# Chunks 6 and 7 with their second layer in seven products, and q and k of units 12 to 23 split by GpSimd's transfers

## The chip, the core and the metric

The kernel runs on one core of a Trainium2 chip. The metric is the time of one execution on the device in microseconds (us). TensorE is called PE, VectorE DVE, ScalarE ACT, GpSimd POOL or Pool, SyncE SP in the profile, and so here.

## The reference

An attention with a narrow band and block summaries feeds a two-layer MLP. B, H, S, D = 4, 8, 768, 64; the MLP goes from 512 to 2048 and back to 512 columns.

```python
k_sum = k.reshape(B, H, nb, block, D).max(axis=3)          # block 32, nb 24
v_sum = v.reshape(B, H, nb, block, D).mean(axis=3)
scores_l = scale * q @ k.T, masked to |i - j| < 16
scores_s = scale * q @ k_sum.T + log(block)
a = softmax(concat([scores_l, scores_s]))
x = a @ concat([v, v_sum])                                  # per head, heads side by side
h = x @ w_in;  g = gelu(h) (erf);  out = g @ w_out          # 3072 tokens
```

## The kernel before, in words

Everything is written out by hand in one list, `ORDER`: each entry names a step with its numbers, a step issues its instructions on its engines' queues when the list comes to it, and each engine then works its own queue in order and waits for semaphores. So the list sets the order within an engine; entries of different engines run past one another.

**Precision.** TensorE multiplies f16. Every factor is held as a sum of two f16 parts (hi and lo), and a product is three matmuls: hi·hi, hi·lo, lo·hi. The hi part is a copy on ACT, the lo part a subtraction on DVE.

**Attention** runs in 24 units (four heads by 256 tokens). For a unit `load_q`, `load_k` fetch f32 tiles on SP's queue, `s_q_hi`, `s_k_hi` (ACT, L796, L739) and `q_lo`, `k_lo` (DVE, L805, L799) split them. k's parts lie in `k_hi[u % 2]` and `k_lo[u % 2]`, so unit u can fill its buffer only when `scores` of unit u-2 is done. Then `scores` (PE, L831, 48 small matmuls), `add_mask` (DVE, L851), `maximum` (an all-reduce over partitions on Pool, L860), `shift`, `exponent`, `s_p_hi`, `p_lo`, `values` (PE, L913), `sums` (PE, L929), and the division and split that give x.

**The MLP** runs in twelve chunks of 256 tokens. Chunks 0 to 3 do the first layer straight (`phase1`, 24 matmuls of 256 columns a step). Chunks 4 to 11 do it in pairs b = 2 to 5, with the seven products of Strassen's scheme (`sp b q n`, L1061, 12 matmuls of 256 columns, q a quarter of the 2048 columns): the sums of input blocks are `xsum`, the sums of weight blocks are made once by `wt_add`, `wt_hi`, `wt_lo` and stay in the tile `wt`. The second layer of chunks 0 to 7 is straight: `phase2 c i`, L1109 to L1111, eight steps a chunk, each 12 matmuls of 512 columns. The second layer of chunks 8 to 11 (pairs 4 and 5, `L2`) is in seven products too: `so b n q j`, L1297, 6 matmuls of 256 columns, 56 steps a pair. For those the hidden blocks are combined by `h_sum` and split by `h_hi`, `h_lo` (L1186, L1189) and the sums of `w_out` blocks are made by `t_sum`, `t_hi`, `t_lo` (L1231, L1236, L1260, L1263) between the steps of chunks 8 and 9, into tiles of attention that are free by then. Pair 5 keeps its combined hidden blocks in `wt`, whose weight sums nobody needs any more.

The end is `so 5 4 3 1`, its evacuation `o_out 5 1` (ACT, L1333) and a store `o_put` on SP's queue (L1337).

Of the kernel before, what the change touches and what calls it, by code (L numbers as in the profile page):

```python
# [16 lines left out]
ALU = mybir.AluOpType  # L17
# [41 lines left out]
M16_ROOM = 0  # L59
# [14 lines left out]
L2 = (4, 5)  # L74
N_FILL = 16
# [50 lines left out]
s_q_hi 10, wt_add 0 0, g_lo 2 0, load_vs 8, v_hi 8, exponent 9, load_k 10, fetch_v 2 0, v_lo 8, load_v 11, phase1 3 4,  # L126
s_k_hi 10, sums 8, g_lo 2 3, scores 11, add_mask 11, load_v 10, wt_add 0 1, values 8, put 0 1, q_lo 10, wt_add 0 2,
phase1 3 5, gelu 3 2, load_vs 10, k_lo 10, norm_take 8, s_p_hi 9, p_lo 9, phase1 3 6, maximum 11, wt_hi 0, norm_cross
8, sums 9, scores 10, norm_rec 8, norm_spread 8, load_q 12, load_k 12, gelu 3 6, store 1 1, norm_mult 8, gelu 3 5,
prep_v 2 0, load_vs 11, x_hi 8, add_mask 10, v_hi 10, values 9, norm_take 9, wt_lo 0, norm_cross 9, g_hi 3 6, put 1 1,  # L130
shift 11, g_hi 3 2, gelu 3 4, s_k_hi 12, v_lo 10, wt_add 2 0, x_lo 8, g_hi 3 4, k_lo 12, s_q_hi 12, fetch_v 2 3,
norm_rec 9, phase1 3 1, q_lo 12, phase1 3 0, v_hi 11, v_lo 11, exponent 11, g_lo 3 2, prep_v 2 3, phase2 2 1, k_sums 2
0, norm_spread 9, s_p_hi 11, load_k 13, gelu 3 1, load_q 13, norm_mult 9, maximum 10, phase1 3 7, load_v 12, phase2 2
3, prep_k_end 2 1, g_lo 3 4, s_q_hi 13, p_lo 11, x_hi 9, shift 10, g_hi 3 1, wt_add 3 0, gelu 3 0, wt_add 3 1, q_lo
13, s_k_hi 13, g_hi 3 0, phase2 2 5, phase1 3 3, g_lo 3 0, wt_add 3 2, k_sums 2 1, wt_add 2 1, sums 11, norm_take 11,
g_hi 3 5, g_lo 3 1, load_vs 12, scores 12, exponent 10, load_v 13, values 11, norm_cross 11, phase2 2 7, wt_add 2 2,
s_p_hi 10, load_q 17, sp 2 0 1, add_mask 12, norm_rec 11, wt_hi 2, k_lo 13, x_lo 9, scores 13, p_lo 10, sums 10, gelu
3 7, load_vs 13, gelu 3 3, norm_spread 11, maximum 12, norm_mult 11, norm_take 10, values 10, sp 2 0 2, s_q_hi 17,
snap 2 0 1, q_lo 17, wt_lo 2, x_hi 11, store 2 1, v_hi 12, x_lo 11, v_lo 12, norm_cross 10, load_k 15, g_hi 3 3, g_lo
3 3, add_mask 13, shift 12, s_k_hi 15, maximum 13, g_lo 3 5, norm_rec 10, exponent 12, v_hi 13, load_q 15, norm_spread  # L140
10, s_q_hi 15, norm_mult 10, xsum 2 1, comb 2 0 0, phase2 2 0, phase2 2 2, phase2 2 4, put 2 1, s_p_hi 12, sp 2 1 1,
k_lo 15, p_lo 12, xsum 2 3, phase2 2 6, sp 2 1 2, xsum 2 2, sums 12, q_lo 15, load_k 14, xsum 2 4, shift 13, load_v
15, values 12, wt_add 4 0, xs_hi 2 1, xs_hi 2 2, g_hi 3 7, xs_hi 2 3, wt_add 4 1, snap 2 1 1, xs_hi 2 4, xs_lo 2 1,
load_vs 15, wt_add 5 0, wt_add 5 1, scores 15, store 2 0, phase2 3 0, g_lo 3 7, exponent 13, norm_take 12, wt_hi 3,
xs_lo 2 3, xs_lo 2 2, load_q 14, norm_cross 12, wt_lo 3, s_gelu 2 0 0, wt_add 4 2, wt_hi 4, phase2 3 2, s_p_hi 13,
norm_rec 12, sp 2 0 6, sp 2 1 6, s_k_hi 14, comb 2 1 0, wt_add 6 0, wt_add 5 2, xs_lo 2 4, wt_add 6 1, sg_hi 2 0 0,
snap 2 0 2, v_hi 15, sp 2 0 5, put 2 0, wt_lo 4, phase2 3 4, g_lo 3 6, wt_hi 5, sp 2 0 7, wt_add 7 0, k_lo 14, v_lo
15, norm_spread 12, snap 2 1 2, phase2 3 6, s_q_hi 14, sp 2 1 7, wt_add 7 1, wt_add 7 2, snap 2 0 3, wt_hi 7, store 3
0, p_lo 13, wt_add 6 2, load_k 17, v_lo 13, wt_hi 6, sp 2 0 4, s_gelu 2 0 2, wt_lo 7, comb 2 0 3, phase2 3 1, wt_lo 5,
load_v 14, wt_lo 6, sp 2 0 3, sg_hi 2 0 2, fetch_v 3 0, put 3 0, sp 2 1 5, load_vs 14, norm_mult 12, prep_v 3 0,  # L150
s_gelu 2 0 3, fetch_k 3 1, sg_lo 2 0 2, phase2 3 3, s_gelu 2 1 0, comb 2 0 1, sp 2 2 1, q_lo 14, load_q 16, sg_lo 2 0
0, s_gelu 2 0 1, s_k_hi 17, k_lo 17, sg_hi 2 1 0, add_mask 15, sg_lo 2 1 0, snap 2 1 3, values 13, snap 2 2 1, comb 2
1 3, s_gelu 2 1 3, sums 13, prep_k 3 1, sg_hi 2 1 3, scores 14, v_hi 14, sp 2 2 6, sg_hi 2 0 3, snap 2 2 2, sp 2 1 3,
sg_lo 2 0 3, load_k 16, v_lo 14, add_mask 14, comb 2 1 1, sp 2 1 4, norm_take 13, maximum 15, phase2 3 5, s_gelu 2 1
2, load_v 17, s_k_hi 16, sg_hi 2 0 1, s_gelu 2 1 1, sg_hi 2 1 1, maximum 14, sg_lo 2 0 1, sp 2 2 2, shift 15, comb 2 2
0, shift 14, norm_cross 13, s_q_hi 16, fetch_v 3 2, q_lo 16, exponent 14, sg_hi 2 1 2, s_p_hi 14, sp 2 3 2, phase2 3
7, norm_rec 13, load_q 18, exponent 15, sp 2 3 1, snap 2 3 1, sg_lo 2 1 3, norm_spread 13, k_lo 16, sg_lo 2 1 1,
fetch_k 3 0, sp 2 2 7, scores 16, p_lo 14, norm_mult 13, load_k 18, comb 2 3 0, values 14, sums 14, store 3 1, sg_lo 2
1 2, norm_take 14, s_p_hi 15, x_hi 12, sp 2 2 5, norm_cross 14, prep_k 3 0, snap 2 2 3, prep_k_end 3 0, sp 2 3 6,
phase2 4 0, snap 2 3 2, p_lo 15, x_hi 13, s_gelu 2 2 0, comb 2 2 3, sp 2 2 3, norm_rec 14, norm_spread 14, sp 2 2 4,  # L160
add_mask 16, norm_mult 14, comb 2 2 1, s_gelu 2 2 3, sp 2 3 5, values 15, s_gelu 2 3 0, scores 17, sg_hi 2 2 0, sums
15, load_v 16, sg_hi 2 3 0, maximum 16, sp 2 3 7, prep_v 3 2, phase2 4 2, sg_lo 2 2 0, s_gelu 2 2 1, fetch_k 3 2, x_lo
13, put 3 1, shift 16, exponent 16, snap 2 3 3, sg_hi 2 2 1, sp 2 3 4, norm_take 15, sg_lo 2 3 0, fetch_k 3 3, comb 2
3 3, prep_k 3 2, s_k_hi 18, norm_cross 15, x_lo 12, s_gelu 2 3 2, sp 2 3 3, sg_hi 2 2 3, s_p_hi 16, sg_lo 2 2 1,
s_gelu 2 3 3, load_vs 16, k_lo 18, sp 3 0 1, norm_rec 15, add_mask 17, sg_hi 2 3 2, comb 2 3 1, sp 3 0 2, norm_spread
15, sg_hi 2 3 3, norm_mult 15, s_q_hi 18, s_gelu 2 3 1, q_lo 18, load_vs 17, v_hi 16, sg_hi 2 3 1, phase2 4 4, v_hi
17, p_lo 16, sg_lo 2 3 1, phase2 4 6, v_lo 16, x_hi 15, maximum 17, k_sums 3 0, scores 18, fetch_v 3 1, s_gelu 2 2 2,
x_lo 15, sg_hi 2 2 2, store 4 0, sg_lo 2 2 3, shift 17, load_k 19, sums 16, load_v 18, xsum 3 1, load_q 20, xs_hi 3 1,
values 16, snap 3 0 1, phase2 5 0, sg_lo 2 3 2, xsum 3 3, fetch_v 3 3, s_k_hi 19, s_q_hi 20, exponent 17, v_lo 17,
xsum 3 2, comb 3 0 0, xs_hi 3 2, prep_k 3 3, norm_take 16, prep_k_end 3 1, sg_lo 2 2 2, sp 3 1 2, sp 3 1 1, prep_v 3  # L170
1, sg_lo 2 3 3, k_lo 19, k_sums 3 1, xs_lo 3 2, phase2 5 2, phase2 5 4, snap 3 1 1, sp 3 0 6, q_lo 20, comb 3 1 0,
s_p_hi 17, xsum 3 4, sp 3 1 6, phase2 5 6, put 4 0, xs_hi 3 4, load_q 19, xs_lo 3 4, load_v 19, xs_lo 3 1, snap 3 0 2,
add_mask 18, xs_hi 3 3, xs_lo 3 3, sp 3 0 7, maximum 18, prep_v 3 3, s_gelu 3 1 0, s_q_hi 19, snap 3 1 2, store 5 0,
shift 18, snap 3 0 3, norm_cross 16, load_k 20, sp 3 0 5, comb 3 0 3, norm_rec 16, exponent 18, load_vs 18, v_hi 18,
sp 3 0 4, norm_spread 16, p_lo 17, sp 3 1 7, norm_mult 16, phase2 4 1, s_k_hi 20, q_lo 19, scores 19, add_mask 19,
s_gelu 3 0 0, s_gelu 3 0 2, values 17, v_lo 18, sums 17, norm_take 17, norm_cross 17, norm_rec 17, put 5 0, maximum
19, sp 3 0 3, phase2 4 3, phase2 4 5, s_gelu 3 0 3, sg_hi 3 0 0, sg_lo 3 0 0, k_lo 20, shift 19, load_k 21, phase2 4
7, norm_spread 17, s_p_hi 18, comb 3 0 1, s_gelu 3 0 1, sg_hi 3 0 1, exponent 19, sp 3 2 1, p_lo 18, sp 3 1 5, s_k_hi
21, snap 3 2 1, snap 3 1 3, store 4 1, sums 18, norm_mult 17, load_q 21, values 18, s_q_hi 21, scores 20, k_lo 21,
norm_take 18, sp 3 2 6, phase2 5 1, load_vs 19, v_hi 19, sg_lo 3 0 1, comb 3 1 3, sp 3 1 3, sg_hi 3 1 0, snap 3 2 2,  # L180
s_p_hi 19, norm_cross 18, sg_lo 3 1 0, q_lo 21, load_v 20, add_mask 20, sg_hi 3 0 3, load_k 22, norm_rec 18, comb 3 1
1, sp 3 1 4, s_k_hi 22, maximum 20, s_gelu 3 1 1, sg_hi 3 1 1, k_lo 22, sg_lo 3 0 3, sp 3 2 7, v_lo 19, sp 3 2 2,
# [71 lines left out]
1  # L254
'''


SLOTS = {
    "f4k": (
        "0123020301321302310302320130310213021302321022013023313020301323012323130230102101312010320231302130"  # L260
        "212130"
    ),
    "g32": (
        "012301203223103123011323320131133012130213021322032100323012320130121032"
    ),
    "ks16": (
# [1185 lines left out]
```

## Time and profile before

| | us |
|---|---|
| median of 3 runs (562.19 to 562.35) | 562.32 |
| profiled execution, span | 560.5 |
| PE busy | 552.6 (99%) |
| DVE busy | 472.6 (84%) |
| ACT busy | 384.8 (69%) |
| Pool busy | 94.7 (17%) |

The span runs from the first to the last instruction that the profile shows; the median stands 1.8 us above it. The granted clock was 1.00, the level of 2.4 GHz, in every slice. Matmuls are pipelined, so a duration of one (379 ns for 512 columns) is longer than its share of PE's time; the time from one start to the next is what counts. The same holds in part for DVE and ACT.

### The profile page before, as it was taken

To read this page: it belongs to the slowest core of one execution; us is meant where nothing else is said; L and a number is where in the kernel's file an instruction comes from. 1 tells how busy PE (TensorE), PEld (TensorE's weight loads), DVE (VectorE), ACT (ScalarE), POOL (GpSimd) and SP (SyncE) were. 2 spreads that over 40 slices of the span, in tenths; PEclk is the share of its full clock that TensorE was granted. 3 is DMA by queue.
4 is the path that set the end of the run, shared out by engine and by line. 5 is a ranking of instruction groups with operands and counts; after the bars stand their busy time and mean duration, and the time that the engine had idled before them with its cause. 6 is when DMAs were issued, how large, how long until landed. Compare 5 with 4: busy or idle time off the path is not lost.

```text
span 560.5 us, 13994 instructions
## 1 busy us (share of the span) xinstructions
PE 552.6 (99%) x6011; PEld 402.2 (72%) x6011; DVE 472.6 (84%) x660; ACT 384.8 (69%) x665; POOL 94.7 (17%) x42
## 2 busy tenths in 40 slices
PE   8999999999999999999999999999999999999997
PEld 4568886585677666677766677665668788888886
DVE  4999999999999999979898768768689999667641
ACT  4689766768688997658878787795747664455521
POOL 2644030202412240031222211223000000000000
PEclk9999999999999999999999999999999999999999
DMA  8989545647554423424352043220000000001011
GB/s 320 396 274 389 189 154 191 266 130 207 158 163 116 146 64 107 144 81 139 91 148 90 28 130 115 63 65 2 22 19 1 20 1 2 2 1 48 1 48 57
DMA packets 29230, 64.30 MB, mean 115 GB/s; under 512 B 2800, under 2 KB 8688, under 8 KB 29168
## 3 DMA queue, kind: packets, MB, share of 16 engines
q1 hardware_dynamic: 28880, 63.06, 34.3%
q8 instruction: 47, 0.77, 0.6%
q10 hardware_dynamic: 288, 0.34, 0.2%
q14 instruction: 15, 0.12, 0.1%
HBM read 55.34 MB, written 6.29 MB: 110 GB/s over the span
## 4 chain that ended last, share of the span: by engine, by line
PE 76%; DVE 17%; DMA 3%; issue 2%; ACT 1%; SPq 0%; DVEq 0%
PE psy L1061 13%; PE pso L1109 9%; PE pso L1110 9%; PE pso L1111 9%; PE psz L1061 7%; PE psd_y L1297 4%; PE pso_y L1297 3%; PE pss_x L1297 3%; PE psx L1061 3%; PE psv L913 3%; PE psh L990 2%; PE psh L991 2%; PE psh L992 2%; PE pss L831 2%; DMA w_out_h<-in_vt_dram 2%
## 5 line engine op out<-in xcount | busy, mean ns | idle before, releaser
L860 POOL PARTITION_ALL_REDUCE m<-s x23 | 82.4, 3582 | 284.4 <-DVE s L851 114.2
L1109 PE MATMUL pso<-w_out_h,gg 128*128 128x512 f16 x256 | 97.1, 379 | 0.0
L1111 PE MATMUL pso<-w_out_h,gg 128*128 128x512 f16 x256 | 97.0, 379 | 0.0
L1110 PE MATMUL pso<-w_out_l,gg 128*128 128x512 f16 x256 | 97.0, 379 | 0.0
L1061 PEld LDWEIGHTS <-wt 128*128 128x128 f16 x768 | 74.7, 98 | 12.1 <-issue 0.6
L991 PE MATMUL psh<-xos,ww 128*128 128x256 f16 x256 | 69.8, 273 | 0.8 <-DVE xos L970 0.8
L990 PE MATMUL psh<-xos,ww 128*128 128x256 f16 x256 | 69.8, 273 | 0.1
L1061 PE MATMUL psy<-xos,wt 128*128 128x256 f16 x576 | 69.8, 273 | 0.0
L992 PE MATMUL psh<-xos,ww 128*128 128x256 f16 x256 | 69.8, 273 | 0.0
L1061 PEld LDWEIGHTS <-ww 128*128 128x128 f16 x576 | 56.0, 98 | 9.8 <-issue 0.2
L1111 PEld LDWEIGHTS <-gg 128*128 128x128 f16 x256 | 25.0, 98 | 30.5 <-DVE gg L1093 0.4
L1109 PEld LDWEIGHTS <-gg 128*128 128x128 f16 x256 | 25.0, 98 | 25.9
L1110 PEld LDWEIGHTS <-gg 128*128 128x128 f16 x256 | 25.0, 98 | 25.8
L1297 PEld LDWEIGHTS <-gg 128*128 128x128 f16 x384 | 37.6, 98 | 5.1 <-issue 0.3
L1072 ACT ACTIVATE ww<-psy 128x512 f32<-128x512 f32 x48 | 27.8, 588 | 13.7 <-PE psy L1061 10.9
L1189 DVE SCALAR_TENSOR_TENSOR gg<-h,gg 128x512 f16<-128x512 f32 x32 | 21.7, 684 | 11.1 <-ACT gg L1186 11.1
L1093 DVE SCALAR_TENSOR_TENSOR gg<-g,gg 128x512 f16<-128x512 f32 x32 | 22.7, 711 | 8.0 <-ACT gg L1089 7.9
L865 DVE TENSOR_TENSOR s<-s,m 128x1024 f32<-128x1024 f32 x21 | 25.5, 1217 | 4.3 <-POOL m L860 4.3
L990 PEld LDWEIGHTS <-ww 128*128 128x128 f16 x256 | 25.0, 98 | 4.2 <-issue 0.2
L992 PEld LDWEIGHTS <-ww 128*128 128x128 f16 x256 | 25.0, 98 | 4.1 <-issue 1.2
L991 PEld LDWEIGHTS <-ww 128*128 128x128 f16 x256 | 25.0, 98 | 3.8
L999 ACT ACTIVATE g<-psh 128x512 f32<-128x512 f32 x32 | 18.9, 593 | 11.4 <-DVE gg L1008 8.7
(192 smaller groups left out, 1273.1 us busy)
## 6 DMA issues: line engine op xcount, KB each, us to landing
v<-in_vw_dram SPq DMA_DIRECT2D x24, 512.0 KB
k<-in_kd_dram SPq DMA_DIRECT2D x20, 320.0 KB
gg<-in_w_in_dram SPq DMA_DIRECT2D x6, 1024.0 KB
q<-in_qd_dram SPq DMA_DIRECT2D x23, 256.0 KB
kp<-in_kp_dram SPq DMA_DIRECT2D x12, 392.0 KB
vb<-in_vb_dram SPq DMA_DIRECT2D x12, 384.0 KB
xos<-in_w_out_dram SPq DMA_DIRECT2D x4, 1024.0 KB
x32s<-in_w_out_dram SPq DMA_DIRECT2D x4, 1024.0 KB
```

Of the source, the lines that this page charges most:

```text
L860: nc.gpsimd.partition_all_reduce(out_ap=self.m32, in_ap=self.s32, channels=P, reduce_op=bass_isa.ReduceOp.max)
L865: nc.vector.tensor_tensor(out=self.s32, in0=self.s32, in1=self.m32, op=ALU.subtract)
L990: nc.tensor.matmul(ph[:, e, :], wh, xh, start=(k == 0), stop=False)
L991: nc.tensor.matmul(ph[:, e, :], wh, xl, start=False, stop=False)
L992: nc.tensor.matmul(ph[:, e, :], wl, xh, start=False, stop=(k == NCC - 1))
L1061: nc.tensor.matmul(ps[:, e, :], ws, xx, start=(first and e == 0 and k == 0 and m == 0), stop=(k == 1 and m == 2), skip_group_check=True,)
L1072: nc.scalar.activation(snaps[b, q, n], split8(acc[b, q, "y"]), AF.Copy)
L1093: nc.vector.scalar_tensor_tensor(out=g_part(o // 2, q, 1, fs), in0=g32t.pop((b, q, o)), scalar=SC_G, in1=g_part(o // 2, q, 0, fs), op0=ALU ...
L1109: nc.tensor.matmul(p, gh, w_out_h[:, f, :], start=(f == 0), stop=False)
L1110: nc.tensor.matmul(p, gh, w_out_l[:, f, :], start=False, stop=False)
L1111: nc.tensor.matmul(p, gl, w_out_h[:, f, :], start=False, stop=(f == NFC - 1))
L1297: nc.tensor.matmul(ps, g, ww_, start=(first and e == 0 and k == 0), stop=(e == 1 and k == 2), skip_group_check=True,)
```

## The change

- `STREAM = (3,)`: the second layer of chunks 6 and 7 (pair 3) is done by 56 steps `so 3 n q j` in place of 16 steps `phase2`. Their hidden blocks take the `h_` steps (`h_comb`, `h_gelu`, `h_sum`, `h_hi`, `h_lo`) in place of `comb`, `s_gelu`, `sg_hi`, `sg_lo`.
- Pair 3 comes before pair 4, whose first layer still needs the weight sums in `wt`, and the combined hidden blocks of pair 3 go into `wt`. So `ws` (4 steps) writes `wt` to DRAM beforehand, and `wr` (16 steps, 256 KB each) reads it back, slot by slot, as the steps `so 3` let go of it. The `w_out` sums are made earlier, staged in one tile and written to DRAM by `ts` (16); `t1_load` (2) and `tl` (12) read them for pair 3, `tr` (12) for pairs 4 and 5. All of these are on SP's queue.
- Units 12 to 23: `q_cast`, `k_cast` are transfers issued by Pool that convert f32 to f16 on the way; ACT writes the negated copy (`q_neg`, `k_neg`); `q_acc`, `k_acc` are transfers by Pool that add the f32 source to it, which leaves the lo part. They take the place of `load_q`, `load_k`, `s_q_hi`, `s_k_hi`, `q_lo`, `k_lo`. A new input `k96` holds k in rows padded to 96 columns; `k_sum` (ACT) writes the block maxima into `k_hi` after each cast.
- The accumulators of pair 3 lie in the `pso` bank and in `psh`; `mask16_sb` and `ks_f` move into a tile that is free early on; `ks16` has four buffers; the scratch for Pool's transfers doubles.
- The order is unchanged up to the 499th entry (the end of `v_lo 8`) and new from there on, with other buffer numbers in `SLOTS`.

The diff, cut; of the new order two places stand: from `scores 10` to shortly before `scores 12`, and the start of pair 4.

```diff
-M16_ROOM = 0
+M16_ROOM = 1
...
+STREAM = (3,)
...
+2 1, wt_add 0 2, norm_take 9, phase1 3 3, load_v 11, scores 10, x_hi 8, load_vs 10, maximum 11, g_hi 3 4, g_lo 2 3,
+load_vs 11, wt_hi 0, shift 11, wt_hi 3, norm_cross 9, add_mask 10, wt_lo 0, values 9, v_hi 11, q_acc 12, phase2 2 1,
+wt_lo 3, put 1 1, k_cast 12, v_hi 10, v_lo 10, norm_rec 9, norm_spread 9, norm_mult 9, k_cast 13, gelu 3 0, exponent
+11, g_lo 3 1, s_p_hi 11, g_hi 3 2, q_cast 13, k_neg 12, fetch_v 2 3, maximum 10, k_sums 2 1, g_lo 3 4, phase1 3 5,
+phase2 2 3, g_hi 3 0, k_acc 12, q_neg 13, p_lo 11, shift 10, k_sum 12, exponent 10, q_acc 13, phase1 3 7, v_lo 11,
+gelu 3 7, wt_add 7 0, wt_add 7 1, sums 11, wt_add 7 2, phase2 2 5, g_hi 3 7, x_lo 8, k_sums 2 0, g_lo 3 0, values 11,
...
+23, wr 3 3 1, sums 21, so 3 4 0 1, wr 3 0 2, wr 3 1 2, xsum 4 4, o_snap 3 3 0, so 3 4 0 0, xs_hi 4 4, sp 4 0 1, snap 4
+1 1, maximum 23, o_sum 3 3, sp 4 0 2, so 3 4 1 1, norm_mult 20, snap 4 0 1, v_lo 21, values 21, wr 3 1 3, wr 3 0 0,
+h_comb 4 0 0, h_gelu 4 0 0, so 3 4 1 0, shift 23, xs_lo 4 4, xs_lo 4 3, sp 4 1 2, exponent 22, load_vs 23, exponent
+23, h_comb 4 1 0, norm_take 21, wr 3 0 1, wr 3 2 2, h_hi 4 0 11, wr 3 1 0, sp 4 0 6, sp 4 0 5, snap 4 0 2, wr 3 2 1,
+s_p_hi 23, sp 4 0 7, wr 3 1 1, p_lo 23, norm_cross 21, sp 4 1 6, snap 4 0 3, sp 4 0 4, v_hi 23, h_lo 4 0 11, norm_rec
+21, v_lo 23, h_comb 4 0 3, snap 4 1 2, sp 4 1 7, h_gelu 4 0 3, sp 4 0 3, norm_spread 21, h_hi 4 0 22, sums 23,
+norm_mult 21, h_gelu 4 0 2, h_lo 4 0 22, h_gelu 4 1 0, so 3 4 2 1, h_sum 4 0 1, sp 4 2 1, h_hi 4 1 11, so 3 4 2 0,
+h_comb 4 0 1, tr 0 4, h_sum 4 0 3, h_sum 4 0 2, values 23, h_hi 4 0 1, snap 4 1 3, sp 4 1 5, h_gelu 4 0 1, norm_take
...
+    dr = ctx.enter_context(tc.tile_pool(name="dr", bufs=1, space=bass.MemoryType.DRAM))
+    t_dram = [dr.tile([P, NQ, 2, 512], F16, name=f"t_dram_{n}") for n in range(4)]
+    wt_dram = dr.tile([P, NFC // 2, 1024], F32, name="wt_dram")
...
-                nc.gpsimd.memset(a[:, :, TQ + NBLK : KW], 0.0)
+                nc.gpsimd.memset(a[:, :, TQ:KW], 0.0)
...
+            if b >= 2 and i == 0:
+                continue
...
+        def q_cast(self):
+            self.qh = wk.tile([P, QCOLS], F16, tag="qh", bufs=N_QH, name=f"qh_{self.nm}")
+            nc.gpsimd.dma_start(out=self.qh, in_=qd[self.u])
+
+        def q_neg(self):
+            self.ql = wk.tile([P, QCOLS], F16, tag="ql", bufs=N_QH, name=f"ql_{self.nm}")
+            nc.scalar.activation(self.ql, self.qh, AF.Copy, scale=-1.0)
+
+        def q_acc(self):
+            nc.gpsimd.dma_start(out=self.ql, in_=qd[self.u], accum_op=ALU.add)
+
+        def k_cast(self):
+            nc.gpsimd.dma_start(out=k_hi[self.u % UPC].rearrange("p t j -> p (t j)"), in_=k96[self.u])
+
+        def k_sum(self):
+            nc.scalar.activation(
+                self.kh[:, :, 0:CT, SLOT_SUM : SLOT_SUM + NBLK],
+                ks16[self.b, self.h0 // UH][:, 0].unsqueeze(2).broadcast_to([P, NR, CT, NBLK]), AF.Copy,
+            )
+
+        def k_neg(self):
+            nc.scalar.activation(self.kl[:, :, :, 0:TQ], self.kh[:, :, :, 0:TQ], AF.Copy, scale=-1.0)
+
+        def k_acc(self):
+            nc.gpsimd.dma_start(out=k_lo[self.u % UPC].rearrange("p t j -> p (t j)"), in_=k96[self.u], accum_op=ALU.add)
...
-        if b == L2[0]:
+        if b == L2[0] and b not in STREAM:
...
+        if b in STREAM and (b, q, o) not in g32t:
+            g32_tile((b, q, o))
...
+    def wt_slot(q, i):
+        return wt[:, 2 * q : 2 * q + 2].rearrange("p i n -> p (i n)")[:, i * 512 : (i + 1) * 512]
+
+    def t_tile(q, n):
+        if (n, q) not in t2w:
...
+    def t_room(b, q, n, z):
+        if n == 1:
+            return b_part(q, 0, 1, z)
+        if b in STREAM:
+            t = wt_slot(q, {2: 3, 3: 2, 4: 0}[n]).bitcast(F16)[:, z * 512 : (z + 1) * 512]
+        else:
+            t = t_tile(q, n)
+            t = t[z] if len(t) > 1 else t[0][:, z * 512 : (z + 1) * 512]
+        return t.rearrange("p (e n) -> p e n", e=2)
+
+    def t1_load(z):
+        dst = (w_out_h, w_out_l)[z].rearrange("p (q e h) n -> p q e h n", q=NQ, e=2)
+        for q in range(NQ):
+            queue[0].dma_start(
+                out=dst[:, q, :, 0, CH : 2 * CH], in_=t_dram[0][:, q, z].rearrange("p (e n) -> p e n", e=2)
+            )
+
+    def tl(b, q, n):
+        queue[0].dma_start(
+            out=wt_slot(q, {2: 3, 3: 2, 4: 0}[n]).bitcast(F16), in_=t_dram[n - 1][:, q].rearrange("p z n -> p (z n)")
+        )
+
+    def tr(q, n):
+        t = t_tile(q, n)
+        src = t_dram[n - 1][:, q].rearrange("p z n -> p (z n)")
+        m = 1024 // len(t)
+        for i, a in enumerate(t):
+            queue[0].dma_start(out=a, in_=src[:, i * m : (i + 1) * m])
+
+    def ws(q):
+        queue[0].dma_start(out=wt_dram[:, 2 * q : 2 * q + 2], in_=wt[:, 2 * q : 2 * q + 2])
+
+    def wr(b, q, i):
+        src = wt_dram[:, 2 * q : 2 * q + 2].rearrange("p i n -> p (i n)")
+        queue[0].dma_start(out=wt_slot(q, i), in_=src[:, i * 512 : (i + 1) * 512])
...
+            if k == 2:
+                return flat2(x32s[:, 4])
+            if ("f", q) not in b12:
+                b12["f", q] = wk.tile([P, WP], F32, tag="f4k", bufs=N_F4K, name=f"tw_{q}")
+            return b12["f", q][:, k * 512 : (k + 1) * 512]
...
+        t = ld.tile([P, KC * TQ], F32, tag="k32", bufs=N_K32, name=f"tst_{q}_{n}")
+        tst[q, n] = t.bitcast(F16)[:, :1024].rearrange("p (z n) -> p z n", z=2)
+        nc.scalar.activation(tst[q, n][:, 0], t32f[n, q], AF.Copy)
 
     def t_lo(q, n):
-        nc.vector.tensor_tensor(out=t_room(q, n, 1), in0=t_src(q, n), in1=t_room(q, n, 0), op=ALU.subtract)
+        nc.vector.tensor_tensor(out=tst[q, n][:, 1], in0=t32f[n, q], in1=tst[q, n][:, 0], op=ALU.subtract)
+
+    def ts(q, n):
+        queue[0].dma_start(out=t_dram[n - 1][:, q], in_=tst[q, n])
...
-        if first:
+        if first and b in STREAM:
+            if y == "y":
+                t = ps_o.tile([P, DM], F32, tag="pso", name=f"pso_y_{b}").rearrange("p (e j) -> p e j", e=2)
+                acc[b, y, 0], acc[b, y, 1] = t[:, 0], t[:, 1]
+            else:
+                t = ps_h.tile([P, 2, CH], F32, tag="psh", name=f"psh_{y}_{b}")
+            acc[key] = t
+        elif first:
...
+    k96[..., :TQ] = kd.reshape(nu, P, KC, TQ)
+    k96 = k96.reshape(nu, P, KC * KW)
...
-    nc = _bacc.Bacc("TRN2", target_bir_lowering=False, num_devices=1, dynamic_dma_scratch_size=512)
+    nc = _bacc.Bacc("TRN2", target_bir_lowering=False, num_devices=1, dynamic_dma_scratch_size=1024)
```

## Rows read from the trace of the kernel before

**Rows 1.** The page: the span, and busy time of each engine.
```profile
span 560.5 us, 13994 instructions
PE 552.6 (99%) x6011; PEld 402.2 (72%) x6011; DVE 472.6 (84%) x660; ACT 384.8 (69%) x665; POOL 94.7 (17%) x42
```
**Rows 2.** Busy time by stretch, 150 to 400 and 420 to 460 us.
```profile
core 0: us, PE busy (x) PEld busy (x) DVE busy (x) ACT busy (x) POOL busy (x), PEclk, DMA share, GB/s
150.00:400.00 250.00, 250.00 (x2996) 168.82 (x2994) 214.25 (x302) 198.82 (x337) 51.98 (x15) 1.00 0.33 98
420.00:460.00 40.00, 40.00 (x333) 32.36 (x331) 39.78 (x66) 27.27 (x51) 0.00 (x0) 1.00 0.02 8
```
**Rows 3.** Waits of PE over the whole span, longest: total, times, longest.
```profile
PE psn L785 <- ACT s L868: 1.0, 1, 1.0
```
**Rows 4.** Timeline of PE: steps following one another (start, duration, instructions).
```profile
303.49 0.38 PE L1109 MATMUL pso<-w_out_h,gg 128*128 128x512 f16 x1
...
306.07 1.47 PE L1061 MATMUL psy<-xos,wt 128*128 128x256 f16 x12
307.38 1.47 PE L1061 MATMUL psz<-xos,wt 128*128 128x256 f16 x12
```
**Rows 5.** Timeline of PE, late: steps of the second layer in seven products.
```profile
556.04 0.82 PE L1297 MATMUL pso_y<-t,gg 128*128 128x256 f16 x6
556.69 0.82 PE L1297 MATMUL psd_y<-t,gg 128*128 128x256 f16 x6
```
**Rows 6.** Timeline of PE where the kind of its work changes.
```profile
313.69 0.38 PE L1111 MATMUL pso<-w_out_h,gg 128*128 128x512 f16 x1
314.00 0.20 PE L831 MATMUL pss<-qh,k_all 64*128 64x64 f16 x2
314.04 0.19 PE L831 MATMUL pss<-ql,k_all 64*128 64x64 f16 x2
...
314.68 0.19 PE L831 MATMUL pss<-qh,k_all 64*128 64x64 f16 x2
314.81 0.22 PE L913 MATMUL psv<-ph,vh 128*64 128x64 f16 x2
```
**Rows 7.** Timeline of DVE in a full stretch.
```profile
430.19 0.68 DVE L1162 TENSOR_TENSOR h<-psz,ww 128x512 f32<-128x512 f32 x1
430.79 0.68 DVE L1183 TENSOR_TENSOR h<-h 128x512 f32<-128x512 f32 x1
```
**Rows 8.** Groups by line and shape: the split of k and q.
```profile
L799 DVE TENSOR_TENSOR k_all<-k,k_all 128x640 f16<-128x640 f32 x20 | 17.6, 879 | 2.9 <-ACT k_all L739 2.9
L805 DVE TENSOR_TENSOR ql<-q,qh 128x512 f16<-128x512 f32 x21 | 14.2, 675 | 1.6 <-ACT qh L796 1.6
L739 ACT ACTIVATE k_all<-k 128x640 f16<-128x640 f32 x20 | 14.5, 724 | 0.2 <-DMA k<-in_kd_dram 0.2
```
**Rows 9.** Timelines of SP and of DMA by stretch around one load of 256 KB.
```profile
333.05 0.33 SPq L666 DMA_DIRECT2D q<-in_qd_dram  x1
...
339.95 1.66 SPq L703 DMA_DIRECT2D v<-vm  x2
...
334.00:336.00 2.00, 2.00 (x21) 1.80 (x19) 1.11 (x4) 1.96 (x4) 1.37 (x1) 1.00 0.35 135
336.00:337.00 1.00, 1.00 (x11) 0.90 (x10) 1.00 (x1) 0.99 (x2) 1.00 (x1) 1.00 0.00 0
```
**Rows 10.** Pool's all-reduces, as a group and two on the timeline; DVE beside them.
```profile
L860 POOL PARTITION_ALL_REDUCE m<-s x23 | 82.4, 3582 | 284.4 <-DVE s L851 114.2
...
143.07 4.58 POOL L860 PARTITION_ALL_REDUCE m<-s  x1 [7.81 <-DVE s L851]
250.76 3.22 POOL L860 PARTITION_ALL_REDUCE m<-s  x1 [3.83 <-issue]
...
144.63 1.97 DVE L527 TENSOR_TENSOR t<-wt,t 128x256 f32<-128x256 f32 x1
252.20 1.01 DVE L1093 SCALAR_TENSOR_TENSOR gg<-g,gg 128x512 f16<-128x512 f32 x1 [0.64 <-ACT gg L1089]
```

## What the change should do to the time

> **What bounds the kernel now.** I read the page's totals first: PE is busy for 552.6 of 560.5 us, DVE for 472.6, ACT for 384.8, Pool for 94.7 [rows 1]. Busy PE need not be PE at work, so the waits come next: the longest wait of PE for anyone is 1.0 us in total [rows 3], and from 150 to 400 us PE is busy for 250.00 of 250.00 [rows 2]. Then the timeline, to see whether its steps follow at the pace of their columns: a `phase2` step of 12 matmuls takes 306.07 - 303.49 = 2.58 us, 0.215 a matmul of 512 columns; an `sp` step of 12 takes 1.31, 0.109 a matmul of 256 [rows 4]; an `so` step of 6 takes 0.65 [rows 5]. 512 columns at 2.4 GHz are 0.213. So PE's stream of columns is the bound from early on to the end, and everything else hides under it. A change is worth what it takes out of that stream, as long as the others still keep up.
>
> **PE's stream: products.** Removed: 16 `phase2` steps of 2.58 = 41.3 us [rows 4]. Added: 56 `so` steps of 0.65 to 0.655 = 36.6 us [rows 5]. Sum -4.7 us. (192 matmuls of 512 columns become 336 of 256: seven eighths of the columns.)
>
> **PE's stream: changes of kind.** The timeline shows a second price. From the start of the last 512-column matmul to that of the first scores matmul is 0.31 us, where a follower of its own kind starts after 0.215: 0.095 more. From scores to values it is 0.13, where a scores matmul gives way after some 0.03 to 0.04: again about 0.095 [rows 6]. Between `phase2` and `sp` it is nothing [rows 4]. So each change among the kinds big matmul, scores, values, sums costs some 0.095 us. I count them in both orders from the entry where they part: 62 before, where scores, values and sums often stand next to one another, and 82 after, where they mostly stand alone between products. 20 x 0.095 = +1.9 us, on the path. PE's stream then is 4.7 - 1.9 = 2.8 us shorter.
>
> **DVE.** On the whole little changes. Removed: 12 `k_lo` of 0.88 and 12 `q_lo` of 0.68 [rows 8], 18.6 us. Added: 16 `h_sum`, 12 more lo steps (28 `h_lo` for 16 `sg_lo`) and 4 `o_sum`, 32 operations of 0.68 [rows 7], 21.8 us. What matters is that 32 `t_sum` and 16 `t_lo` move from beside chunks 8 and 9 to before them. Up to the first step of chunk 8 the new order has some 82 more of the 512-column operations, which start 0.60 us apart [rows 7], 49 us, less 11 `k_lo` and 12 `q_lo`, 15 us: +34. DVE had 250 - 214 = 36 us idle from 150 to 400 [rows 2], and the 50 `so` steps (32.5) less two `phase2` (5.2) and plus one `sp` (1.3) that are now ahead of chunk 8 make that stretch 29 us longer. So 36 + 29 - 34 = 31 us of 279 stay idle: 89% full. That a fuller DVE does not stop PE is shown at 420 to 460: DVE 39.8 of 40, PE 40.0 [rows 2]. I put it at nothing; the cover is those 31 us.
>
> **ACT.** Each removed `s_k_hi` (0.72, [rows 8]) has a `k_neg` of its size, each `s_q_hi` a `q_neg`; 28 `h_hi` for 16, and `k_sum`, add about 12 us to an engine with 51 of 250 us idle [rows 2]. Nothing.
>
> **SP's queue and the reloads.** About 75 transfers are added, 0.33 us of SP each [rows 9], 25 us over some 300: room enough, but SP waits in order, so a `ts` that waits for `t_lo`, or a `tr` that waits for a buffer, holds all behind it. One 256 KB load lands in under 3 us: issued at 333.05, its traffic is over by 336 [rows 9]. The tightest place is the start of pair 4. `wr 3 0 0` may go when `so 3 4 0 0` is done; behind it on SP stand `load_vs 23`, two transfers of 0.83 [rows 9], and `wr 3 0 1`, which `sp 4 0 6` needs as well: 0.33 + 1.66 + 0.33 + 3 = 5.3 us. PE has three `sp`, two `so` steps and `values 21` in between: 3 x 1.31 + 2 x 0.65 + 0.9 + two changes of kind = 6.3. For quarter 1 it is 0.7 + 3 = 3.7 against four `sp`, 5.2. It fits, by 1.0 and 1.5 us; four quarters, and the `tl` loads, are as near. I allow 0.5 us of PE waits for all of them, from zero (all fit) to 4 x 1 us (each lands 2 to 2.5 us later than the row).
>
> **Pool's transfers.** No row shows one. The nearest from below is SP's issue, 0.33 us [rows 9], from above an all-reduce, 3.6 us [rows 10]. 48 are 16 to 173 us on a Pool that was busy 52 of 250 [rows 2]; the place decides. The tightest is unit 12. Its `k_cast` waits for `scores 10`; then Pool has `k_cast 12`, `k_cast 13`, `q_cast 13`, `maximum 10`, `k_acc 12`, and the last must land before `scores 12`. With P for a transfer that is 4P + 3.6 + 3. PE has three `phase2`, two `phase1` steps (24 matmuls each, 2.62), two `values` and `sums` between: 7.7 + 5.2 + 2.0 = 15 us. So P up to 2.1 us costs nothing. I take P near 1, as its job, a list of 128 rows, is SP's and not the all-reduce's: 0 us, with the wait of 6 us at P = 3.6 for the range. The Trainium skill ("DMA: Bandwidth & Descriptors", Latency and other measured facts) gives about 1 us to the first byte for such a transfer, 0.6 for SP's; no run here shows the former. By it the sum stays as it is.
>
> **Sum.** -4.7 + 1.9 + 0.5 = -2.3 us on the profiled execution: 560.5 to 558.2. The end (last `so`, `o_out`, `o_put`) and the 1.8 us outside the span stay, so 562.3 - 2.3 = **560.0 us**.
>
> **Rivals.**
> 1. The reloads are late. For: margins of 1.0 to 1.5 us, an SP queue that stalls in order, and loads in a stretch that had little traffic. Against: 98 GB/s on average in rows 2, so engines are free. Price 2 to 4 us: 562.
> 2. Pool's transfers are slow: the mechanism that ends slower. Place: `scores 12` first, then every unit whose buffer is refilled within some 20 us, and all-reduces queued behind a transfer. Price: at P = 3.6, 14.4 + 6.6 = 21 against 15 is 6 us at unit 12 alone: 559.5 + 6 = 565.5 or more. It decides from P = 2.1; slower than before by over 1.1 us from P = 3.1.
> 3. DVE is held up by Pool. Beside an all-reduce a 256-column operation took 1.97 us, and a 512-column one 1.01 for 0.68 [rows 10]. If a transfer does so too, 48 x 0.33 = 16 us go under the 31 idle ones, but from 0.65 each DVE is full, and at 1 us each PE waits 17 us: 576. The Trainium skill ("SBUF — State Buffer", Who interferes with whom) says that DVE operations with two SBUF inputs collide with Pool instructions that read SBUF, and not with those that only write. By that rule the transfers, which read no tensor on Pool, hold up nothing; the row agrees as far as the all-reduce reads.
> 4. The changes of kind cost nothing more, as the new neighbours hide them: 557.7 to 558.
>
> **How the numbers follow.** Forecast (waits 0 to 1.7 us, 559.5 to 561.2): 0.52. Rival 1 and other waits of that size: 0.18. Rival 2: 0.17. Rival 3: 0.08. Rival 4: 0.05. What a measurement of this kernel can tell from no change is about 0.2%, 1.1 us. Faster: 0.52 + 0.05 = 0.57; same (561.2 to 563.4): 0.18; slower: 0.25. The range leaves out rival 4 below and the upper part of rivals 2 and 3, some 0.15: 558.4 to 566.5.
>
> **What would show it.** The matmul lines must hold 576 of 512 columns at L1109 to L1111's successors and 1008 `so` matmuls. Where scores follow a big matmul the gap of 0.095 must appear 82 times, and PE's stretch from 150 us on must have no wait over 1 us. Rival 1 shows as PE waiting for DMA `wt`, rival 2 for DMA `k_all` or as ACT waiting for casts, rival 3 as DVE durations above 0.68 beside Pool. The forecast is wrong if the span is above 560 with PE waits of over 3 us in it, or if a transfer of Pool is over 2.1 us.

## The result, and the profile after

| kernel | us, median | against before, with its 95% interval | profiled span, us |
|---|---|---|---|
| before | 562.26 (561.96 to 562.35) | | 560.5 |
| after | 570.66 (568.60 to 571.11) | 1.0144 [1.0126, 1.0161] | 569.3 |

The forecast was 560.0 us, a gain; the change costs 8.4 us (1.4%). The page's totals after, to be laid beside [rows 1], with its DMA queues, its chain of work that ended last, and the median time from issue to landing of Pool's transfers into `k_all`:

```profile
PE 551.6 (97%) x6155; PEld 414.7 (73%) x6155; DVE 484.2 (85%) x668; ACT 391.2 (69%) x685; POOL 128.6 (23%) x90
...
q1 hardware_dynamic: 37104, 75.91, 39.5%
q0 software_dynamic: 6912, 9.05, 13.1%
...
PE 42%; DVE 35%; DMA 12%; issue 5%; ACT 4%; SPq 1%; POOL 0%; DVEq 0%; ACTq 0%; POOLq 0%
...
k_all<-in_k_dram POOLq DMA_DIRECT2D x24, 240.0 KB, 5.5
```

PE has gaps now. Over the stretch of [rows 2] (columns as there):

```profile
150.00:400.00 250.00, 243.33 (x2883) 169.82 (x2881) 235.57 (x336) 197.59 (x349) 78.06 (x62) 1.00 0.64 150
```

PE lost 6.7 us there, DVE is 94% busy, the DMA engines' share went from 0.33 to 0.64. The waits of PE from 150 us on, longest first, against [rows 3]:

```profile
PE psn L980 <- DVE pl L931: 1.9, 2, 1.0
PE psy L1112 <- ACT g L1137: 1.1, 1, 1.1
PE psv L964 <- DVE x32s L1014: 1.0, 1, 1.0
PE psy L1112 <- ACT ww L1123: 0.9, 1, 0.9
PE pso_y L1399 <- ACT g_os L1421: 0.8, 2, 0.5
PE pss_x L1399 <- DVE g_os L1428: 0.8, 1, 0.8
```

No large wait, and none directly for a transfer: a dozen of up to 1.1 us, each for an evacuation or a split that DVE or ACT did late. So I measured PE's stream itself, from a step just ahead of the place where the orders part (`phase1 3 2`, at 156.7 us before and 156.5 after) to the start of the last matmul: 400.5 us before, 409.05 after. "Waits" below are the sum, over that stretch, of what each step starts or ends later than its own pace and the 0.095 us of a change of kind allow: 1.4 us before, 12.8 after. Without them the stream is 399.1 us before and 396.3 after. "Held" is what DVE's operations with two inputs in SBUF, from 150 to 420 us, last longer than the median of their operation and shape, where that is over 0.08 us. From "the same, two staging tiles" on, the mended orders have two staging tiles.

| kernel | us, median | against before | waits, us | held, us |
|---|---|---|---|---|
| before | 562.26 | | 1.4 | 1.9 |
| after | 570.66 | 1.0144 [1.0126, 1.0161] | 12.8 | 9.4 |
| no all-reduces | 566.62; again 563.70 | 1.0061 [1.0030, 1.0092]; 1.0038 [1.0020, 1.0057] | 6.3 | 0.0 |
| no transfers by Pool | 564.81 | 1.0045 [1.0031, 1.0059] | 6.7 | 7.0 |
| transfers that nobody waits for | 569.55 | 1.0148 [1.0127, 1.0168] | 10.5 | 10.2 |
| two staging tiles | 568.91 | 1.0111 [1.0087, 1.0136] | 9.0 | 9.4 |
| small streams | 567.41 | 1.0089 [1.0067, 1.0110] | 8.8 | 8.8 |
| neither all-reduces nor transfers | 561.04 | 0.9985 [0.9970, 1.0000] | 4.9 | 0.0 |
| order mended | 567.39 | 1.0093 [1.0067, 1.0119] | 9.7 | 6.5 |
| the same, two staging tiles | 566.04 | 1.0068 [1.0049, 1.0086] | 8.9 | 6.5 |
| order mended twice | 564.51 | 1.0044 [1.0032, 1.0057] | 6.3 | 6.5 |
| three times | 562.25 | 1.0009 [1.0000, 1.0018] | 4.0 | 6.5 |
| four times | 564.10 | 1.0033 [1.0013, 1.0053] | 3.6 | 6.5 |
| that, no transfers | 562.97 | 1.0017 [1.0007, 1.0027] | 4.9 | 6.0 |
| before, with Pool's split alone | 588.90 | 1.0457 [1.0422, 1.0492] | | 4.6 |

Waits and holds are those of the profiled execution, the time is the median of all, and the runs of one kernel differ by up to 6 us; so a row's numbers need not match. The first median without all-reduces leaves out one slow execution of 946.61 us, at a mean granted clock of 0.56; with it, it is 566.85. From the first mended order on the holds stay the same; what falls is the waits.

**Three threads lead back from these waits.** First, DVE beside Pool's all-reduces. Timeline of Pool and of DVE after, twice (start, duration):

```profile
299.40 3.22 POOL L911 PARTITION_ALL_REDUCE m<-s  x1 [2.50 <-DVE s L902]
...
299.46 2.36 DVE L1355 TENSOR_TENSOR tst<-tw,tst 128x512 f16<-128x512 f32 x1 [0.17 <-ACT tst L1352]
301.75 0.24 DVE L1003 RECIPROCAL rc<-rc 128x16 f32<-128x16 f32 x1
302.03 0.71 DVE L1007 STREAM_TRANSPOSE dent<-rc 128x512 f32<-128x512 f32 x1
...
385.01 0.86 POOL L842 DMA_DIRECT2D ql<-in_qd_dram  x1 [5.89 <-DVE rc L1003]
385.58 3.49 POOL L911 PARTITION_ALL_REDUCE m<-s  x1
...
385.42 0.69 DVE L1014 TENSOR_TENSOR x32s<-psv,dent 128x512 f32<-128x512 f32 x1
386.02 2.26 DVE L1355 TENSOR_TENSOR tst<-x32s,tst 128x512 f16<-128x512 f32 x1
```

`t_lo` has two inputs in SBUF; it takes 0.68 us elsewhere and 2.3 here. The order before mostly puts operations of another sort beside an all-reduce (a transpose, and one with an input in PSUM), and they take their usual time:

```profile
281.06 3.22 POOL L860 PARTITION_ALL_REDUCE m<-s  x1 [8.90 <-DVE s L851]
...
281.41 0.70 DVE L956 STREAM_TRANSPOSE dent<-rc 128x512 f32<-128x512 f32 x1
282.14 0.69 DVE L963 TENSOR_TENSOR x32s<-psv,dent 128x512 f32<-128x512 f32 x1
```

Second, ACT held up in its queue by a landing. Its timeline, and its waits for DMA from 150 to 420 us (total, times, longest):

```profile
170.32 0.63 ACT L839 ACTIVATE ql<-qh 128x512 f16<-128x512 f16 x1 [4.24 <-DMA qh<-in_qd_dram]
170.85 0.58 ACT L1167 ACTIVATE ot<-pso 128x512 f32<-128x512 f32 x1
171.33 1.05 ACT L927 ACTIVATE ph<-s 128x1024 f16<-128x1024 f32 x1
...
ACT tst L1352 <- DMA t_dram<-tst: 7.5, 4, 2.9
ACT ql L839 <- DMA qh<-in_qd_dram: 4.2, 1, 4.2
ACT vh L936 <- DMA v<-vm: 3.0, 2, 2.0
```

`q_neg 12` stands ahead of `s_p_hi 9` and waits 4.2 us for its cast to land; `p_lo 9` on DVE and `sums 9` on PE wait behind it, 1.65 us of PE. All of ACT's waits for DMA there are 16.6 us; before they were 2.2.

Third, the DMA engines. From 219 to 229 us, queue by queue (packets, MB, share of 16 engines), and the chain in that stretch:

```profile
q0 software_dynamic: 439, 0.63, 57.9%
q1 hardware_dynamic: 595, 1.09, 32.6%
...
222.75 5.01 DMA vb<-in_vb_dram
227.76 0.02 issue
227.78 1.22 DVE vs L665
...
DVE vs L665 <- DMA vb<-in_vb_dram: 1.7, 2, 1.2
```

0.63 MB of Pool's casts and accumulates take more of the engines than 1.09 MB of plain transfers. The source of `prep_v 3 0` takes 5.0 us to land, from its issue at 222.75 us; DVE has other work for most of that and stands still for the last 1.2 us (the last line, DVE's waits for it from 150 to 420 us: total, times, longest).

### The profile page after: what moved, and what is told of

It is laid out like the page before. It is cut to its first block, busy times and chain, and to the rows that moved or that the text cites. A ratio compares the mean times of both kernels' runs of the same rounds, so it can differ in the third digit from the quotient of the medians.

```text
span 569.3 us, 14476 instructions
## 1 busy us (share of the span) xinstructions
PE 551.6 (97%) x6155; PEld 414.7 (73%) x6155; DVE 484.2 (85%) x668; ACT 391.2 (69%) x685; POOL 128.6 (23%) x90
## 3 DMA queue, kind: packets, MB, share of 16 engines
q1 hardware_dynamic: 37104, 75.91, 39.5%
q0 software_dynamic: 6912, 9.05, 13.1%
## 4 chain that ended last, share of the span: by engine, by line
PE 42%; DVE 35%; DMA 12%; issue 5%; ACT 4%; SPq 1%; POOL 0%; DVEq 0%; ACTq 0%; POOLq 0%
PE psy L1112 7%; PE pso_y L1399 6%; PE pss_x L1399 4%; PE psz L1112 4%; PE psd_y L1399 4%; DVE s L916 2%; DMA vb<-in_vb_dram 2%; PE pso L1160 2%; DMA v<-in_vw_dram 2%; PE psx L1112 2%; PE psv_z L1399 2%; PE pso L1161 2%; PE pso L1162 2%; DVE tst L1355 2%; DVE gg L1059 2%
## 5 line engine op out<-in xcount | busy, mean ns | idle before, releaser
L1112 PEld LDWEIGHTS <-wt 128*128 128x128 f16 x768 | 74.4, 98 | 12.6 <-issue 2.0
L1160 PE MATMUL pso<-w_out_h,gg 128*128 128x512 f16 x192 | 73.0, 380 | 0.6 <-ACT ot L1167 0.6
L1162 PE MATMUL pso<-w_out_h,gg 128*128 128x512 f16 x192 | 72.9, 380 | 0.6 <-DVE gg L1144 0.6
L1161 PE MATMUL pso<-w_out_l,gg 128*128 128x512 f16 x192 | 72.9, 379 | 0.0
L1399 PEld LDWEIGHTS <-wt 128*128 128x128 f16 x288 | 27.9, 98 | 4.0 <-issue 0.5
L931 DVE TENSOR_TENSOR pl<-s,ph 128x1024 f16<-128x1024 f32 x18 | 22.9, 1274 | 8.4 <-ACT ph L927 8.4
L919 ACT ACTIVATE s<-s 128x1024 f32<-128x1024 f32 x21 | 22.1, 1056 | 6.4 <-DVE s L916 6.2
```

Of the source, the lines that this page charges most:

```text
L919: nc.scalar.activation(self.s32, self.s32, AF.Exp, scale=QKSCALE)
L931: nc.vector.tensor_tensor(out=self.pl, in0=self.s32, in1=self.ph, op=ALU.subtract)
L1112: nc.tensor.matmul(ps[:, e, :], ws, xx, start=(first and e == 0 and k == 0 and m == 0), stop=(k == 1 and m == 2), skip_group_check=True,)
L1160: nc.tensor.matmul(p, gh, w_out_h[:, f, :], start=(f == 0), stop=False)
L1161: nc.tensor.matmul(p, gh, w_out_l[:, f, :], start=False, stop=False)
L1162: nc.tensor.matmul(p, gl, w_out_h[:, f, :], start=False, stop=(f == NFC - 1))
```

## The experiments

My theories: S, two-input operations of DVE held by all-reduces; T, Pool's transfers land late; D, the streams through DRAM. The later runs set "places in the queues" against "DVE is short of time as a whole".

**No all-reduces.**

```diff
-            nc.gpsimd.partition_all_reduce(
-                out_ap=self.m32, in_ap=self.s32, channels=P, reduce_op=bass_isa.ReduceOp.max
-            )
+            nc.gpsimd.memset(self.m32, 64.0)
```

> The changed kernel, with the all-reduce of each of the 24 units replaced by a memset of its output on Pool (the maximum over the scores is left out: a constant is subtracted in its place). The memset reads no SBUF. Theory S (VectorE is full, and its operations with two SBUF inputs are held beside Pool's all-reduces: 9.3 us of stretch from 150 to 420 us in the changed kernel, 1.8 us in the one before): the stretch goes to under 1 us, PE's waits fall from 12.8 us to about 5, time 562 to 566 us. Theory T (Pool's transfers land late): 569 to 571, as their issue and landing stay. Theory D (the streams through DRAM delay what others wait for): 569 to 571.

It gave 566.62 us, then in a second series, from which its trace is, 563.70:

> The kernel without all-reduces once more, for its trace: 566.9 us. By the holds: VectorE's stretch under 0.5 us, the waits of PE at 302, 334 and 388 us (1.1 at the sums of unit 20) gone or under half; those at 169 (q_neg behind its transfer), 408, 418 and 554 us stay.

The same `t_lo` beside a memset on Pool (its rows here):

```profile
291.91 1.28 POOL L911 MEMSET m<- 128x1024 f32 x1
...
292.42 0.69 DVE L1353 TENSOR_TENSOR tst<-tw,tst 128x512 f16<-128x512 f32 x1 [0.17 <-ACT tst L1350]
```

The second median lies in S's range, the first just above it. Held time is 0.0 us, the waits at 302, 334 and 388 us are gone, and those at 408, 418 and 554 stay, as S expected; but the one at 169 us went too, which S had put down to T alone. In this trace `phase1 3 2` starts 2.3 us sooner, a gain ahead of the parting that has nothing to do with the change (the run with neither, below, doesn't show it). The holds are real, and not all of it. By the Trainium skill ("SBUF — State Buffer", Who interferes with whom) a DVE instruction with two SBUF inputs collides with a Pool instruction that reads SBUF, not with one that only writes; the two fences agree.

**No transfers, and transfers that nobody waits for.** For each of the four kinds (the second diff on top of the first):

```diff
-            nc.gpsimd.dma_start(out=self.qh, in_=qd[self.u])
+            nc.gpsimd.memset(self.qh, 0.01)
```
```diff
+            nc.gpsimd.dma_start(out=dead["qh", self.u], in_=qd[self.u])
```

> The changed kernel, with the 48 cast and accumulate transfers of units 12 to 23 replaced by memsets of the same tiles on Pool (the fetch of q and k of these units is left out: constants stand in their place). Pool stays about as busy, nothing has to land, and some 8 MB of traffic are gone. Theory T (the landing of 5 us and ScalarE held up by it): 561 to 565 us. Theory S: only the waits that the trace puts down to q and k go, 1.65 us at the sums of unit 9 and 0.5 at the scores of unit 12: 567.5 to 569.5. Theory D: 568 to 570.

> The changed kernel with constants for q and k of units 12 to 23, as in the run without transfers, and 48 transfers of the same sources issued by Pool at the same places, into DRAM, that nobody waits for (fetch of q and k left out as to the result). If it is the wait for the landing that costs: 564.7 to 566 us, as without transfers. If it is their traffic, which delays the other loads: 567.5 to 570.

Without transfers 564.8 us: T. The stretch from 150 to 400 us there:

```profile
150.00:400.00 250.00, 248.62 (x2978) 174.86 (x2977) 239.26 (x340) 199.74 (x352) 80.06 (x62) 1.00 0.37 117
```

With transfers into DRAM that nobody waits for, 569.55 again, in the range for traffic; this speaks against the wait for their landing as the main cost. In that kernel DVE still waits 2.6 us for `vb` and ACT 5.7 for the stores from staging, against none and 2.5 without transfers. It is no clean split: these transfers cast and don't accumulate, Pool is 20 us busier in the stretch than without transfers, and DVE is held 3.2 us longer. What part of the price is traffic is not shown.

**Two staging tiles; small streams.**

```diff
+        if len(tst) % 2:
+            t = ld.tile([P, QCOLS], F32, tag="q32", bufs=N_Q32, name=f"tst_{q}_{n}")
```
```diff
-        queue[0].dma_start(out=wt_slot(q, i), in_=src[:, i * 512 : (i + 1) * 512])
+        queue[0].dma_start(out=wt_slot(q, i)[:, :64], in_=wt_dram[:, 2 * q, :64])
```

> The changed kernel, with two staging tiles for the sums of w_out blocks in turn (the second is q's f32 tile, free after unit 11), so that the next copy on ScalarE need not wait until the store before it has landed; nothing is left out. ScalarE waited 7.5 us for that in four waits. Theory D: these waits are what PE waits for in the end: 565 to 568 us. Theory S: 569 to 571, ScalarE has room. Theory T: 569 to 571.

> The changed kernel, with one eighth of the columns moved by ws, wr, tl and t1_load (most of the saving and reloading of weight sums for pairs 3 and 4 is left out; ts and tr stay whole). Some 10 MB of 14 that the streams move are gone, the issues on SyncE and their waits stay. Theory D (traffic delays the loads of v, of its block sums and of q and k): 562 to 567 us. Theory S: 568.5 to 570.5. Theory T (Pool's transfers are slow by themselves): 568.5 to 570.5.

-1.75 and -3.25 us, both just above D's ranges and below those of S and T. Each theory has a part, and the single gains (5.9, 4 to 7, 3.3, 1.8) sum to more than the 11.4 us of waits: they eat in part the same slack.

**Neither all-reduces nor transfers.** Both edits together.

> The changed kernel with both: no all-reduces (a constant in the place of the maximum) and no transfers by Pool for units 12 to 23 (constants in the place of q and k). If VectorE's holds and the late transfers are two causes beside each other, the gains add: 570.7 - 3.8 - 5.8 = 561.1 us (560.3 to 562). If both only eat the same slack of VectorE, most of the second gain is gone: 563.5 to 565.

561.04, in the range for two causes beside each other, since 3.8 (from 566.85) and 5.9 us add up to the 9.6 gained. With the second median of the run without all-reduces (7.0 for 3.8) they would not, and in the traces they don't: the waits fall by 6.5 us without all-reduces, by 6.1 without transfers, and by 7.9 without both. So in PE's stream both eat in part the same slack.

**The order mended.** Up to the fourth order nothing is left out: each is a permutation of the changed kernel's 1944 entries. The first of four steps, with what moved:

```diff
-q_neg 12, add_mask 11, store 1 1, phase1 3 4, s_p_hi 9,
+add_mask 11, store 1 1, phase1 3 4, s_p_hi 9, q_neg 12,
...
-q_acc 15, comb 2 0 0, xsum 2 4, load_vs 15, store 2 0, k_neg 14, maximum 13,
+comb 2 0 0, xsum 2 4, load_vs 15, store 2 0, k_neg 14, maximum 13, q_acc 15,
...
-o_sum 5 1, so 5 2 2 1, o_put 5 1 1, so 5 7 2 0, so 5 7 1 0,
+o_sum 5 1, so 5 7 2 0, so 5 7 1 0, so 5 2 2 1, o_put 5 1 1,
```

> The changed kernel in another order, nothing left out: q_neg 12 behind s_p_hi 9 on ScalarE; three all-reduces ahead of the accumulate transfers on Pool that wait for ScalarE (units 13, 17, 21); operations with one SBUF input moved beside all-reduces (norm_rec 17, norm_spread 17 and 20 in, t_lo 1 3 out); o_snap 3 1, o_snap 3 3 0 and snap 4 0 2 earlier on ScalarE; sp 4 0 1, so 5 7 2 0 and so 5 7 1 0 put between a snapshot and the step that waits for it. If the waits come from places in the queues, those that the trace names go (1.65 at the sums of unit 9, 1.6 at so 3 6 0 0 and the sums of unit 20, 0.85 at so 3 4 0, 1.1 at sp 4 0 7, 0.95 at so 5 2 2 1, and some of those after 280 us), 6 us or more: 563 to 565 us. If VectorE as a whole is short of time, they come back at the next step that wants VectorE, and only the 2.9 us from 400 us on are gained: 567 to 569.

> That order and two staging tiles in turn for the sums of w_out blocks. By places in the queues: ScalarE's waits for stores (7.5 us) go as well, worth 1.7 us in the changed kernel: 561 to 563.5 us. By VectorE's shortage: 566 to 568.

567.4 and 566.0, within the second expectation each time. The named waits went or shrank, but others came, in the second kernel 2.85 us at `sp 2 1 7` and 1.7 at `sp 2 2 1`. Their chain led to `prep_v 3 0`, whose source now took 8.2 us to land; DVE stood still for 4.3 us of that (the next text takes the 8.2 for DVE's wait). So once more:

> The changed kernel with two staging tiles and the order mended once more, nothing left out: prep_v 3 0 and wt_add 5 0 behind t_sum 0 2 and wt_add 6 2 on VectorE (it stood still for 8.2 us there, until the block sums' source had landed); so 3 4 2 ahead of sp 4 0 6; s_p_hi 23 and v_hi 23 behind the snapshots that PE waits for. By places in the queues: the 6.8 us of waits that the trace of the former order names go, and the 4.7 - 1.9 us of the products come out: 559.3 to 561 us, below the kernel before. By VectorE's shortage: waits come back elsewhere, 563 to 566.

> The order mended a third time, nothing left out: s_p_hi 23, p_lo 23 and h_comb 4 0 3 earlier (VectorE stood still for 5.9 us behind p_lo 23), wt_hi 4 behind s_gelu 2 0 2, store 4 0 behind k_sums 3 0, sg_lo 2 2 3 out of the all-reduce of unit 17. By places in the queues: the five waits left in that trace (0.9 at sp 2 2 1, 0.63 at phase2 5 0, 0.57, 1.41 and 0.74 after the scores of unit 23), 4.2 us, go: 560 to 561.5 us, at or below the kernel before. By VectorE's shortage: at most the three at the end go, and waits come back in between: 562 to 564.

564.5, then 562.25: the three steps took back all of the loss but what these runs can't tell, 1.0009 [1.0000, 1.0018] against before; the order by 3.3, 1.5 and 2.3 us, the second staging tile by 1.4. All four times so far (567.4, 566.0, 564.5, 562.25) lie within the second expectation, the one for DVE's shortage, so the times by themselves do not decide against it; the stretch shown below does.

> The mended order with sp 4 2 2 ahead of sp 4 1 3, so that PE doesn't wait 0.74 us for h_comb 4 1 3; nothing left out. By places in the queues: 561.3 to 561.7 us, 0.1% below the kernel before. By VectorE's shortage: the wait moves on, 562.1 to 562.5.

> That order without the transfers of units 12 to 23 (memsets of constants in their place; the fetch of q and k left out). If their traffic costs in any order: 3 to 5 us less, 556.5 to 558.5. If it cost because the order left no room for it: 0 to 1.5 us less, 560 to 561.5, the floor being 559.3 by the sum of the products and the changes of kind.

The wait of 0.74 moved on, to `sp 2 2` of pair 4 (0.63), as the second expectation said, but the median, 564.1 with runs from 561.8 to 565.9, is above both ranges; three steps gave 561.8 to 563.7. Why the fourth is slower in the median stays open: its profiled execution is its fastest. Without transfers that order took 562.97, above the range of 560 to 561.5, above three steps' median and below four's. So in an order that leaves them time, the transfers cost nothing that these runs can tell. The stretch from 150 to 400 us with four steps:

```profile
150.00:400.00 250.00, 249.87 (x2991) 176.03 (x2989) 240.27 (x342) 200.00 (x352) 82.06 (x62) 1.00 0.65 153
```

DVE is fuller than in the changed kernel (240.3 us for 235.6), DMA's share is the same, and PE is at work for 249.9 of 250. So DVE is not short of time there as a whole; what costs is where things stand in the queues. No version that does all the work beat the kernel before.

**Pool's split alone, in the kernel before.** Each cast right behind the `scores` that free its tiles, negation and accumulate some entries later, by a rule and not by hand.

> The kernel before with one half of the change alone: q and k of units 12 to 23 split by Pool's transfers, the second layer of chunks 6 and 7 as before. Each cast stands right behind the scores that free its tiles, the negation some 18 to 30 entries later, the accumulate behind it. If the transfers cost by themselves (landing 5 us, traffic): 563.5 to 568 us. If they cost only where VectorE is 95% full: 561.5 to 563, as VectorE has 18.6 us less to do and PE is full.

588.9, far above both. It tells nothing of the transfers' price in a fair order: PE waits 7.5 us for `k_all` and 9.4 for ACT, which itself waits 7.1 us for a cast with PE's evacuations behind it. It does show how dear a transfer in the wrong place is, and that here a long wait costs twice, since the granted clock was lower during and after it. By stretch:

```profile
185.00:190.00 5.00, 5.00 (x24) 2.22 (x23) 3.86 (x7) 0.00 (x1) 4.05 (x2) 1.00 0.98 122
190.00:195.00 5.00, 0.10 (x1) 0.00 (x0) 1.56 (x2) 2.87 (x4) 0.00 (x0) 0.80 0.33 102
195.00:200.00 5.00, 4.63 (x23) 3.23 (x23) 3.19 (x6) 4.94 (x10) 0.00 (x0) 0.52 0.08 20
200.00:205.00 5.00, 5.00 (x121) 3.06 (x120) 4.33 (x8) 4.61 (x9) 1.13 (x2) 1.00 0.42 67
```

## Why the prediction was wrong, point by point

The step that failed is PE's waits in the sum: 0.5 us for the reloads, and nothing for DVE, ACT and Pool's transfers, as each has idle time enough. The stream got 2.8 us shorter as forecast; the waits came to 12.8 us against 1.4, which is 11.4 more. By its own sign (a span above 560 us with over 3 us of PE waits) the forecast is wrong.

- **PE's stream: right.** Three lines of 192 matmuls of 512 columns are left of three of 256. Products -4.7 and changes of kind +1.9 gave -2.8 us; the stream without waits is 399.1 before and 396.3 after, -2.8. The trace has 83 changes of kind there, 82 were counted, and 0.095 us each fits them. Rival 4 is out.
- **DVE at nothing: the step that failed first.** Two things were wrong in it. The idle time was put at 31 of 279 us; from 150 to 429 us 21 were left, and most of the difference is the 7.5 us more that went into holds. And the proof that a fuller DVE doesn't stop PE was taken from 420 to 460 us [rows 2], where Pool does nothing and DMA's share is 0.02, so that neither all-reduce nor landing disturbs it. The claim itself stands in the mended order, with DVE 96% busy; it does not stand for every order.
- **Rival 3 had the mechanism and the wrong agent.** The row of 1.97 us and the rule were there [rows 10], and I priced the hold for the transfers only. 38 two-input operations of DVE that ran beside transfers alone lasted no longer than others of their shape (-0.2 us in all). What I left out is that the new order puts other operations beside the all-reduces that were there already: 10 are held, for 9.4 us, against 4 and 1.9.
- **ACT at nothing: failed.** I compared busy time with idle time. ACT has room, but it works in order, and a negation that waits 4.2 us for a landing holds what stands behind it. The removed `s_q_hi` waited for loads too, yet these were issued far ahead; a cast can't be before its tile is free.
- **Pool's transfers: P right, landing and place wrong.** A transfer keeps Pool for 0.69 to 0.99 us (means of the four kinds), as taken. It lands after 5.1 to 5.5 us (medians), not 3. At `scores 12`, the place that I called tightest, this cost 0.5 us; the price, 5.9 us in this order, came elsewhere: by ACT's waits, and, as far as the run with transfers that nobody waits for tells, more by the DMA engines. So rival 2's time (565.5 or more) was nearer than the forecast, and its mechanism, a slow Pool, was not what happened.
- **"98 GB/s, so engines are free": failed.** I read the rate and not the share. From 150 to 400 us the transfers raise the share of the DMA engines from 0.37 (without them) to 0.64, and the rate from 117 to 150 GB/s only.
- **SP's reloads: right where I looked.** PE never waits for `wt` in the changed kernel, so rival 1 is out as it stood. The margin was thin all the same: in the first two mended orders PE waited 1.9 and 1.3 us for a reload. Not in the sum were the stores from the one staging tile, for which ACT waits 7.5 us (1.75 us of time), and the streams' traffic (3.25 us).
- **"Order new" as an edit at no cost:** the largest omission. Every term was worked out for an amount of work; the loss lies in the places. Three rounds of moving entries, and a second staging tile, took back 8.4 of 8.4 us. Of the 2.8 us, the last order's profiled execution shows where they went: 2.2 us of waits above the kernel before's are left, at four places after 378 us, and its span is 0.5 us below the 560.5 before. Why the median of that order is 2.3 us above this execution is open.

## What to carry to other kernels

A kernel that is full on PE and ordered by hand has an order that covers its disturbances; a new order has to cover them again. So when a change brings a new order, list the disturbers (instructions that hold another engine, transfers that something waits for in a queue) and look up, for each, what stands beside and behind it; idle time summed over a stretch doesn't answer that. Read the DMA engines' share and not their rate, and take the proof that an engine may run full from a stretch that has the same disturbers in it.

## What the runs showed of the hardware that I had not expected

- In the changed kernel an operation of DVE of 512 columns with two SBUF inputs that starts early in an all-reduce ends some 2.4 to 2.7 us behind the all-reduce's start, whenever it started (2.36 us long at 0.06 us, 2.08 at 0.34, 1.26 at 1.13, for 0.68); the all-reduce itself lasts 3.2 to 3.7 us. So the hold covers its first 1.7 to 2.0 us for these, and up to 2.6 us for others in these runs. An operation with one input can be held too, and later: a cast of 128x48 that started 2.7 us into the all-reduce at 249.1 us took 0.91 us for 0.18 and ended with it. The Trainium skill ("SBUF — State Buffer", Summary: rules for kernel authors) has the second one block until the first is done; here the measurement decides.
- Casting and accumulating transfers moved 9.05 MB in 13.1% of the 16 engines' span, plain ones 75.91 MB in 39.5%: 2.8 times the engine time for a byte as the profile counts them (bytes written, for the casts).
- In the kernel with Pool's split alone PE stood still from 190.1 to 195.4 us; the granted clock was 0.80 from 190 to 195 and 0.52 from 195 to 200 us, so some 2 + 4.8 us at the level of 1.2 GHz, most of them behind the wait, and 2.4 GHz (1.00) from 200 to 205 us.
